# Attention and feed-forward on one core: eight sink keys in place of sixteen, and one transposed sink tile for two pairs of heads

## The chip, the cores and the metric

One core of a Trainium2 chip runs the whole program in one launch. The metric is the device time of one execution in microseconds (us). The 128 x 128 matrix engine is TensorE, shown as PE in the profile, with its weight loads shown apart as PEld. VectorE is DVE, ScalarE is ACT, GpSimd is POOL, and SyncE is SP, whose queue issues all the transfers.

## The reference

```python
scores = q @ k.T / sqrt(64)                # 4 batches, 8 heads, 768 positions, head size 64
keep   = (key < n_sink) | ((0 <= query - key) & (query - key < window))   # n_sink 4, window 128
a      = exp(scores - max) over the kept keys; a = a / (sum(a) + 1e-9)
x      = (a @ v), heads side by side       # 3072 tokens x 512
h      = x @ w_in                          # 512 x 2048
g      = s * max(h, 0)**2 + b
out    = g @ w_out                         # 2048 x 512
```

So each query block of 128 sees its own key block, the one before it, and the first four keys, the sinks. All is 32-bit float.

## The kernel before, in words

The 3072 tokens are eight chunks of 384 (`ORDER`: a batch and a half of its sequence). While TensorE does the feed-forward of chunk c, the attention of chunk c + 1 is laid between its steps. A value that needs more than TensorE's fast 32-bit form keeps is split into a high part and a rest, so one product costs two or three matmuls.

**The feed-forward** (`moe_steps`) of a chunk has 32 steps: for each of 16 slices f, `l1(f)` makes `h` with 12 matmuls of 384 columns (L598), and `l2(f)` adds nine matmuls of 512 columns into three output banks (L617). Between them ScalarE takes the relu into tile `r` (L601), VectorE squares it in place (L603), ScalarE makes the high part of `g` (L605) and VectorE the rest (L606), which is the last reader of `r`. `l2(f)` stands two slices behind `l1(f)`. `r` has two buffers.

**Attention.** Chunks 0 and 1 use a plain form. Chunks 2 to 7 use the blocked form, whose work is cut into slots, one for each unit: a head and a block of 128 queries, 24 units a chunk, two heads to a pair. `unit_a` makes scores of 272 columns: two key blocks and 16 sink keys between or after them (144 for the first block of a sequence), with two matmuls, `kh` (L303) and `kl` (L304). VectorE masks and takes the maximum (L308), ScalarE the exponential (L314), GpSimd adds the two key blocks into one (L317) and copies the sinks' exponentials three times into `psk` (L318). A few slots later `turn` transposes the sum (L324), `unit_b` parts and splits it (L337 to L340), and `unit_c` multiplies with the values (L368, L376).

**Sinks and 1/sum.** The sinks' part of the output and the factor 1/sum come for a whole pair at once. `psk` holds, for the three query blocks of a pair, the sinks' exponentials (96 rows after the transpose) and 1/sum in two parts (rows 96 to 99). At the end of a pair, three transposes bring it into bank `ts` (L390), ScalarE and VectorE move it to `xsk` (L392, L393). `sinks` then does one matmul `os` with the sink values `vs` (L399), `scaled` one matmul `zb` with the selector `sel` (L406), and L407 to L409 write the pair's `x`, which the next chunk's `l1` reads.

**What sets the order.** `attn_slots` writes down in which slot each piece stands: `LB` and `LC` slots after a unit's scores, and `LD` or, for the last pair, `LDL` for `sinks` and `scaled`. The loop at the end of the file deals the slots out over the steps by the line below, so that a step takes one slot or, here and there, two. A scheduler may still move instructions that do not depend on each other.

```python
            while i < len(slots) and i * (len(steps) - 2 * (c > 0)) < (j + 1) * len(slots):
```

The banks `sc`, `o`, `ts`, `os`, `zb` and `h` go round in one pool of five.

Of the kernel before, what the change touches and what calls it, by code (L numbers as in the profile page):

```python
# [40 lines left out]
def tile_kernel(ctx, tc, qT, kT, k0, v, vsk, n_sink, window, w, s, b, out):  # L41
# [15 lines left out]
    m_all = const.tile([P, 6 * P], MDT, tag="m", name="m_all")  # L57
# [30 lines left out]
    sel = const.tile([P, P], F32R, tag="sel", name="sel")  # L88
# [44 lines left out]
    def constants2():  # L133

        spread = wk.tile([P, P], F32, tag="y", name="spread", bufs=2)
        nc.gpsimd.memset(spread, 0.0)
        for j in range(2):
            nc.gpsimd.affine_select(
                out=spread[96:P].rearrange("p (a d) -> p a d", a=2), in_=spread[96:P].rearrange("p (a d) -> p a d", a=2),
                pattern=[[1, 2], [0, D]], compare_op=ALU.not_equal, fill=1.0, base=2 * j, channel_multiplier=-1)  # L140
# [98 lines left out]
    def load_pair(k, pr):  # L239
# [4 lines left out]
        nkb, k0, kw, v0 = 3 + half, (0, 288)[half], (416, 544)[half], half * 2  # L244
# [28 lines left out]
    def prep_head(k, h):  # L273
# [6 lines left out]
        hd.kh = wk.tile([P, 544], F32R, tag="kh", name="kh")  # L280
        hd.kl = wk.tile([P, 544], F32R, tag="kl", name="kl")
# [10 lines left out]
    def unit_a(k, h, i, sc):  # L292
# [25 lines left out]
        nc.gpsimd.tensor_copy(out=pp.psk[:, i, :6 * NS].rearrange("p (t x) -> p t x", t=3)[:, :, hh * NS:(hh + 1) * NS],  # L318
# [7 lines left out]
    def unit_b(k, h, i, tp):  # L326
# [18 lines left out]
        if h % 2 == 1 and i == BLK - 1:  # L345
            zr = wk.tile([P, 2, BLK, 2], F32, tag="zr", name="zr")
# [4 lines left out]
            nc.gpsimd.tensor_copy(out=pp.psk[:, :, 96:98], in_=zh.bitcast(F32))  # L351
            nc.vector.tensor_tensor(out=pp.psk[:, :, 98:100], in0=zr[:, 1], in1=zh.bitcast(F32), op=ALU.subtract)

    def unit_c(k, h, i):
# [24 lines left out]
        if i == BLK - 1:  # L379
            a, c = (0, D) if h % 2 == 0 else (D, 0)  # L380
            if h % 2 == 0:
                pp.x = wk.tile([P, CH + P], F32, tag="y", name="y", bufs=2)
            nc.scalar.copy(pp.x[a:a + D], hd.o[c:c + D])
            nc.vector.tensor_tensor(out=pp.x[a:a + D], in0=hd.o[a:a + D], in1=pp.x[a:a + D], op=ALU.add)
            if h % 2 == 1:
                nc.gpsimd.tensor_tensor(out=pp.x[:, CH - P:CH], in0=pp.x[:, CH - P:CH], in1=pp.x[:, CH:], op=ALU.add)
# [4 lines left out]
                pp.xs = wk.tile([P, CH], F32R, tag="xsk", name="xsk", bufs=1)
# [10 lines left out]
    def scaled(k, pr):  # L402
# [8 lines left out]
    def attn_slots(c):  # L411
        k = new_chunk(c)
        units, ahead = [], {}
        for pr in range(H // 2):
# [172 lines left out]
    def moe_steps(x, store, wk, before=None, last=False):  # L587
# [3 lines left out]
        def l1(f):  # L591
# [179 lines left out]
    for c in range(NC_):  # L771
# [5 lines left out]
        for j, st in enumerate(steps):  # L777
# [56 lines left out]
```

## Time and profile before

| | |
|---|---|
| Median of 3 runs | 738.36 us (737.77 to 741.83) |
| The profiled execution, its own time | 739.34 us |
| Its span in the profile | 737.2 us |
| Mean granted TensorE clock | 0.977 |
| TensorE matmuls, busy | 704.9 us (96%) |
| VectorE, ScalarE, GpSimd busy | 516.1, 480.0, 396.3 us (70%, 65%, 54%) |

The profiled execution took 2.1 us more than its span: that lies before the first and behind the last instruction of the program. Matmuls overlap in the profile (the end of one is modelled and lies behind the start of the next), so the time that one takes from the next is read from start to start, or from the chain of work that ended last, and not from its own length.

### The profile page before, as it was taken

To read this page: it belongs to the slowest core of one execution; us is meant where nothing else is said; L and a number is where in the kernel's file an instruction comes from. 1 tells how busy PE (TensorE), PEld (TensorE's weight loads), DVE (VectorE), ACT (ScalarE), POOL (GpSimd) and SP (SyncE) were. 2 spreads that over 40 slices of the span, in tenths; PEclk is the share of its full clock that TensorE was granted. 3 is DMA by queue.
4 is the path that set the end of the run, shared out by engine and by line. 5 is a ranking of instruction groups with operands and counts; after the bars stand their busy time and mean duration, and the time that the engine had idled before them with its cause. 6 is when DMAs were issued, how large, how long until landed. Compare 5 with 4: busy or idle time off the path is not lost.

```text
span 737.2 us, 11878 instructions
## 1 busy us (share of the span) xinstructions
PE 704.9 (96%) x3848; PEld 622.0 (84%) x3848; DVE 516.1 (70%) x1213; ACT 480.0 (65%) x1169; POOL 396.3 (54%) x641
## 2 busy tenths in 40 slices
PE   6788899899999999999999999999999999999996
PEld 3367677789988999999998999999999999989895
DVE  6779999738984788757785588847886589743331
ACT  5978888568774787656884677746775677633222
POOL 2254555348991689616773589816775389710000
PEclk9879989999999999999999999999999999999998
DMA  7844122041210212111121222111111212000001
GB/s 280 337 171 193 33 102 72 15 139 51 80 63 31 84 55 65 34 61 54 46 64 44 82 63 64 46 54 49 56 53 45 84 42 59 12 18 26 1 1 47
DMA packets 27221, 53.01 MB, mean 72 GB/s; under 512 B 3472, under 2 KB 15376, under 8 KB 25232
## 3 DMA queue, kind: packets, MB, share of 16 engines
q1 hardware_dynamic: 27152, 52.18, 21.2%
q8 instruction: 32, 0.52, 0.3%
q14 instruction: 37, 0.30, 0.1%
HBM read 45.88 MB, written 6.29 MB: 71 GB/s over the span
## 4 chain that ended last, share of the span: by engine, by line
PE 79%; DVE 10%; DMA 3%; ACT 3%; POOL 2%; issue 1%; SPq 1%; POOLq 0%; ACTq 0%; DVEq 0%
PE po L617 32%; PE h L598 32%; PE o L376 3%; PE sc L303 2%; PE sc L304 2%; PE sc L324 2%; DMA vf<-in_v 2%; DMA w<-in_w 2%; DVE w L214 2%; DVE g L606 1%; DVE wt L213 1%; PE ts L390 1%; POOL w L216 1%; DVE smf L528 1%; DVE r L603 1%
## 5 line engine op out<-in xcount | busy, mean ns | idle before, releaser
L598 PE MATMUL h<-x,w 128*128 128x384 f32 x1536 | 299.8, 344 | 1.1 <-ACT tf L542 0.8
L617 PE MATMUL po<-w,g 128*128 128x512 f32 x1152 | 298.0, 404 | 0.0
L598 PEld LDWEIGHTS h<-x,w 128*128 128x128 f32 x1536 | 268.6, 189 | 6.7 <-ACT tf L542 1.1
L617 PEld LDWEIGHTS po<-w,g 128*128 128x128 f32 x1152 | 212.4, 191 | 45.0 <-issue 2.7
L603 DVE SCALAR_TENSOR_TENSOR r<-h,sb,r 128x384 f32<-128x384 f32 x128 | 78.6, 614 | 82.5 <-ACT r L601 82.2
L606 DVE SCALAR_TENSOR_TENSOR g<-r,sb,g 128x384 fp32r<-128x384 f32 x128 | 102.0, 797 | 39.0 <-ACT g L605 38.2
L340 POOL TENSOR_TENSOR hl<-two,hl 128x256 fp32r<-128x256 f32 x128 | 99.3, 776 | 21.4 <-ACT hl L339 18.2
L601 ACT ACTIVATE r<-h 128x384 f32<-128x384 f32 x128 | 62.3, 487 | 66.7 <-PE h L598 66.5
L605 ACT ACTIVATE g<-r,sb 128x384 fp32r<-128x384 f32 x128 | 78.7, 615 | 34.1 <-DVE r L603 32.8
L317 POOL TENSOR_TENSOR sm<-sm 128x128 f32<-128x128 f32 x128 | 68.0, 531 | 59.5 <-ACT sm L314 55.5
L314 ACT ACTIVATE sm<-sm,negm 128x272 f32<-128x272 f32 (+1 forms) x144 | 73.1, 507 | 35.4 <-DVE negm L308 31.0
L308 DVE CUSTOM_DVE_ANT_0 sm<-sc,msk 128x272 f32<-128x272 f32 (+1 forms) x144 | 60.4, 419 | 40.4 <-PE sc L304 32.6
L284 POOL TENSOR_TENSOR kl<-kraw,kh 128x544 fp32r<-128x544 f32 (+1 forms) x48 | 63.1, 1315 | 21.7 <-ACT kh L282 21.7
L339 ACT CAST hl<-two 128x256 fp32r<-128x256 f32 x128 | 50.6, 395 | 31.6 <-DVE two L337 31.6
L216 POOL TENSOR_TENSOR w<-w 128x1024 int32<-128x1024 int32 (+1 forms) x17 | 32.6, 1919 | 45.6 <-DVE w L214 25.1
L337 DVE TENSOR_TENSOR two<-sc,split 128x256 f32<-128x256 f32 x128 | 53.0, 417 | 4.4 <-POOL hl L340 4.2
L318 POOL COPY psk<-sm 128x48 f32<-128x48 f32 x144 | 40.7, 282 | 26.7 <-ACT sm L314 26.1
L289 POOL TENSOR_TENSOR vv<-vraw,vv 128x256 fp32r<-128x256 f32 (+1 forms) x48 | 34.4, 718 | 24.6 <-ACT vv L288 24.6
L376 PE MATMUL o<-hl,vv 128*128 128x256 f32 (+1 forms) x256 | 44.5, 276 | 0.0
L303 PE MATMUL sc<-kh,qs 128*128 128x272 f32 (+1 forms) x144 | 42.6, 298 | 0.0
L376 PEld LDWEIGHTS o<-hl,vv 128*128 128x128 f32 x256 | 39.6, 189 | 2.9
L304 PE MATMUL sc<-kl,qs 128*128 128x272 f32 (+1 forms) x144 | 41.3, 288 | 0.0
(129 smaller groups left out, 904.4 us busy)
## 6 DMA issues: line engine op xcount, KB each, us to landing
w<-in_w SPq DMA_DIRECT2D x15, 1024.0 KB, 9.0
kraw<-in_kT SPq DMA_DIRECT2D x32, 272.0 KB, 2.6
out<-ot SPq DMA_DIRECT2D x24, 256.0 KB, 2.0
qraw<-in_qT SPq DMA_DIRECT2D x24, 192.0 KB, 2.4
vraw<-in_v SPq DMA_DIRECT2D x16, 256.0 KB, 2.7
kraw<-in_kT SPq DMA_DIRECT2D x16, 208.0 KB, 2.4
vsraw<-in_vsk SPq DMA_DIRECT2D x24, 64.0 KB, 2.0
vraw<-in_v SPq DMA_DIRECT2D x8, 192.0 KB, 2.4
```

What stands on the lines that cost most here:

```text
L284: nc.gpsimd.tensor_tensor(out=hd.kl[:, :kw], in0=hd.k[:, :kw], in1=hd.kh[:, :kw].bitcast(F32), op=ALU.subtract)
L308: nc.vector.tensor_tensor_reduce(out=sm[:, :n], in0=sc[:, :n], in1=m, scale=-0.125, scalar=BIG, op0=ALU.add, op1=ALU.min, accum_out=negm[: ...
L314: nc.scalar.activation(sm[:, :n], sm[:, :n], AF.Exp, bias=negm[:, uu], scale=-1.0, accum_out=pp.zz[:, i, hh:hh + 1])
L317: nc.gpsimd.tensor_tensor(out=sm[:, c1:c1 + P], in0=sm[:, p1:p1 + P], in1=sm[:, c1:c1 + P], op=ALU.add)
L340: nc.gpsimd.tensor_tensor(out=lo, in0=both, in1=hi.bitcast(F32), op=ALU.subtract)
L376: nc.tensor.matmul(hd.o[:, q0:q0 + n * P], hd.vv[:, kb, :], hd.hl[:, t, c0 * P:(c0 + n) * P], start=(hd.n == 0), stop=(i == BLK - 1 and kb ...
L598: nc.tensor.matmul(h[:, :CH], weight[f][:, 0, wi, cc * P:(cc + 1) * P], x[xi][:, cc, :], start=(i == 0), stop=(i == 11))
L601: nc.scalar.activation(r, h[:, :CH], AF.Relu, scale=1.0 / WUP)
L603: nc.vector.scalar_tensor_tensor(out=r, in0=h[:, :CH], scalar=sw_ap, in1=r, op0=ALU.mult, op1=ALU.mult)
L605: nc.scalar.activation(gg[:, 0, :], r, AF.Identity, bias=b_ap, scale=1.0)
L606: nc.vector.scalar_tensor_tensor(out=gg[:, 1, :], in0=r, scalar=b_ap, in1=gg[:, 0, :].bitcast(F32), op0=ALU.add, op1=ALU.subtract)
L617: nc.tensor.matmul(po[tb], gg[:, gi, tsl], weight[f][:, 1, wi, :], start=(f == 0 and i == 0), stop=(f == NF - 1 and i == 2))
```

## The change

The blocked form now keeps eight sink keys for each head. Scores have 264 columns (136 for the first block), and the score masks, key loads and the sinks' share of `psk` shrink with them. Two pairs now share one `psk`: the sinks' exponentials of four heads fill the 96 rows that two heads filled, and 1/sum of four heads fills rows 96 to 103. So the three transposes, the bank `ts` and its two moves come once for two pairs; `sel` becomes two selectors. `sinks` and `scaled` of a pair wait for the second pair of its two, `LD` and `LDL` give each of the two its own slots, and `load_sinks` moves from two slots ahead of a pair to eleven behind its start. The pairs' `x` tiles (`y`) have three buffers, and `r` has one; in the first chunk's feed-forward every second `r` takes the buffer of `xsk`. Chunks 1 to 6 have 34 slots for 29 of the 32 steps; they had 33 for 30.

```diff
-NS = 16
+NS = 8
-RB, VB = 2, 2
+RB, VB = 1, 2
-LB, LC, LD, LDL, L2 = 4, 7, (3, 4), (2, 2), 2
+LB, LC, LD, LDL, L2 = 4, 7, ((3, 4), (6, 7)), ((2, 2), (3, 3)), 2
...
-    sel = const.tile([P, P], F32R, tag="sel", name="sel")
+    sel = const.tile([P, 2, P], F32R, tag="sel", name="sel")
...
-        pp.psk = psks[(k.c * (H // 2) + pr) % 2]
+        pp.psk = psks[(k.c * (H // 4) + pr // 2) % 2]
...
-            c0, n = ((0, 272), (128, 272), (272, 272))[i]
+            c0, n = ((0, W), (P, W), (W, W))[i]
...
-        nc.gpsimd.tensor_copy(out=pp.psk[:, i, :6 * NS].rearrange("p (t x) -> p t x", t=3)[:, :, hh * NS:(hh + 1) * NS],
+        nc.gpsimd.tensor_copy(out=pp.psk[:, i, :12 * NS].rearrange("p (t x) -> p t x", t=3)[:, :, h % 4 * NS:(h % 4 + 1) * NS],
...
-                pp.x = wk.tile([P, CH + P], F32, tag="y", name="y", bufs=2)
+                pp.x = wk.tile([P, CH + P], F32, tag="y", name="y", bufs=3)
...
+            if h % 4 == 3:
                 ts = ps("ts")
                 for j in range(BLK):
                     nc.tensor.transpose(ts[:, j * P:(j + 1) * P], pp.psk[:, j, :], ident)
-                pp.xs = wk.tile([P, CH], F32R, tag="xsk", name="xsk", bufs=1)
+                pp.xs = k.pairs[h // 2 - 1].xs = wk.tile([P, CH], F32R, tag="xsk", name="xsk", bufs=1)
...
-        nc.tensor.matmul(zb[:, :CH], sel, pp.xs, start=True, stop=True)
+        nc.tensor.matmul(zb[:, :CH], sel[:, pr % 2], pp.xs, start=True, stop=True)
...
-            todo = ((-5, load_pair, pr), (-5, load_keys, h), (-2, load_sinks, pr), (-2, prep_head, h), (-2, load_keys, h + 1),
+            todo = ((-5, load_pair, pr), (-5, load_keys, h), (11, load_sinks, pr), (-2, prep_head, h), (-2, load_keys, h + 1),
...
-            t = 2 * BLK * (pr + 1) - 1 + LC
-            for d, fn in zip(LD if pr < H // 2 - 1 else LDL, (sinks, scaled)):
+            t = 4 * BLK * (pr // 2 + 1) - 1 + LC
+            for d, fn in zip((LD if pr < H // 2 - 2 else LDL)[pr % 2], (sinks, scaled)):
...
-            r = wk.tile([P, CH], F32, tag="r", name="r", bufs=RB)
+            r = wk.tile([P, CH], F32, tag="xsk" if before and f % 2 else "r", name="r", bufs=RB)
...
-            while i < len(slots) and i * (len(steps) - 2 * (c > 0)) < (j + 1) * len(slots):
+            while i < len(slots) and i * (len(steps) - 3 * (c > 0)) < (j + 1) * len(slots):
```

Three places show how instructions now stand on an engine. Lines in the changed kernel are numbered two higher from L347 on (L392 is the transposes' L390, L401 and L408 are `os` and `zb`, L600 and L619 are `l1` and `l2`).

TensorE, in the middle of a chunk, where the first pair of heads ends; before:

```order
L368 MATMUL o<-hl,vv 128x256
L376 MATMUL o<-hl,vv 128x256 x2
L390 MATMUL ts<-identr,psk_96 128x128 x3
L303 MATMUL sc<-kh,qs 128x272
L304 MATMUL sc<-kl,qs 128x272
L324 MATMUL sc<-identr,sm 128x128
```

In the changed kernel, TensorE a little later in the same chunk, where the first pair's `os` and `zb` (sinks and 1/sum) now stand, in a step that takes two slots:

```order
L377 MATMUL o<-hl,vv 128x256 x2
L377 MATMUL o<-hl,vv 128x128 x2
L303 MATMUL sc<-kh,qs 128x264
L304 MATMUL sc<-kl,qs 128x264
L324 MATMUL sc<-identr,sm 128x128
L369 MATMUL o<-hl,vv 128x256
L377 MATMUL o<-hl,vv 128x256 x2
L303 MATMUL sc<-kh,qs 128x264
L304 MATMUL sc<-kl,qs 128x264
L401 MATMUL os<-xsk,vs 128x384
L324 MATMUL sc<-identr,sm 128x128
L600 MATMUL h<-x_2_1391,w_944 128x384
```

The transposes of the first pair are gone (its `psk` is turned with the second pair's), and its `os` stands behind two slots that follow each other without a feed-forward step between them.

TensorE at the end of a chunk, behind the 12 matmuls of `l1` for the last slice but those named; before:

```order
L617 MATMUL po<-w_1132,g 128x512 x9
L399 MATMUL os<-xsk,vs 128x384
L406 MATMUL zb<-xsk,sel 128x384
L617 MATMUL po<-w_1193,g 128x512 x9
L617 MATMUL po<-w_1267,g 128x512 x9
L598 MATMUL h<-x_3_2485,w_415 128x384
```

In the changed kernel (the last pair's `os` and `zb` and what follows, up to the next chunk's first `l1`):

```order
L600 MATMUL h<-x_2_1391,w_1271 128x384
L401 MATMUL os<-xsk,vs 128x384
L408 MATMUL zb<-xsk,sel 128x384
L619 MATMUL po<-w_1136,g 128x512 x9
L619 MATMUL po<-w_1197,g 128x512 x9
L619 MATMUL po<-w_1271,g 128x512 x9
L600 MATMUL h<-x_3_2475,w_419 128x384
```

Three runs of nine `l2` matmuls now lie between the last `zb` and the next chunk's `l1`, where two lay.

ScalarE at the start of a chunk, from the relu of slice 1 to that of slice 2 (`r`), with the casts of the sink values (`vs`); before:

```order
L601 ACTIVATE r<-h 128x384
L279 CAST qs<-qraw 64x384
L270 CAST vs<-vsraw 128x128
L314 ACTIVATE sm,zz<-sm,negm 128x272
L605 ACTIVATE g<-r,sb 128x384
L282 CAST kh<-kraw 128x544
L601 ACTIVATE r<-h 128x384
```

In the changed kernel:

```order
L603 ACTIVATE r<-h 128x384
L279 CAST qs<-qraw 64x384
L314 ACTIVATE sm,zz<-sm,negm 128x264
L282 CAST kh<-kraw 128x528
L607 ACTIVATE g<-r,sb 128x384
L270 CAST vs<-vsraw 128x128 x2
L603 ACTIVATE r<-h 128x384
```

The relu of slice 2 stands behind both first casts of sink values, where before one of them stood ahead of it and one behind. It now writes the one buffer of `r`, which slice 1 has to leave first.

## Rows read from the trace of the kernel before

**Rows 1.** The page: busy time of each engine; the chain that ended last, by engine.

```profile
PE 704.9 (96%) x3848; PEld 622.0 (84%) x3848; DVE 516.1 (70%) x1213; ACT 480.0 (65%) x1169; POOL 396.3 (54%) x641
PE 79%; DVE 10%; DMA 3%; ACT 3%; POOL 2%; issue 1%; SPq 1%; POOLq 0%; ACTq 0%; DVEq 0%
```

**Rows 2.** Busy us by stage: window, length, PE, PEld, DVE, ACT, POOL, clock, DMA.

```profile
0.00:54.00 54.00, 39.98 (x201) 24.09 (x202) 38.92 (x135) 39.13 (x91) 18.88 (x28) 0.84 0.69 265
54.00:133.00 79.00, 68.25 (x347) 53.54 (x345) 76.63 (x130) 62.68 (x120) 42.08 (x26) 0.93 0.26 96
133.00:234.53 101.53, 101.18 (x561) 91.21 (x561) 71.51 (x167) 68.59 (x173) 65.77 (x110) 0.98 0.22 66
234.53:320.27 85.74, 85.67 (x486) 78.73 (x485) 63.78 (x150) 59.08 (x151) 59.30 (x103) 1.00 0.19 57
320.27:403.56 83.29, 83.29 (x469) 76.52 (x469) 59.38 (x150) 56.30 (x151) 47.90 (x87) 1.00 0.18 57
```

**Rows 3.** The chain that ended last, 234 to 326 us: start, us, what.

```profile
261.21 0.24 PE o L376 x2
...
267.58 0.33 PE ts L390 x3
267.91 0.12 PE sc L303
268.03 0.13 PE sc L304
268.16 0.11 PE sc L324
...
320.09 0.18 PE zb L406
320.27 4.18 PE po L617 x18
```

**Rows 4.** The chain again, 324 to 332 us, where a 144-column pair stands.

```profile
326.56 0.07 PE sc L303
326.63 0.11 PE sc L304
326.74 0.17 PE sc L303
326.91 0.13 PE sc L304
```

**Rows 5.** TensorE in order of time: start, length, line, operation.

```profile
296.99 0.29 PE L304 MATMUL sc<-kl,qs 128*128 128x272 f32 x1
297.36 0.33 PE L324 MATMUL sc<-identr,sm 128*128 128x128 f32 x1
```

**Rows 6.** Groups by line: busy us, mean ns | idle before, releaser.

```profile
L598 PE MATMUL h<-x,w 128*128 128x384 f32 x1536 | 299.8, 344 | 1.1 <-ACT tf L542 0.8 <-DVE xsk L393 0.3
L393 DVE TENSOR_TENSOR xsk<-ts,xsk 32x384 fp32r<-32x384 f32 x24 | 13.2, 550 | 0.7
L407 DVE TENSOR_TENSOR y<-zb,y 128x384 f32<-128x384 f32 x24 | 13.2, 548 | 0.6
L408 ACT CAST x<-y 128x384 fp32r<-128x384 f32 x24 | 12.2, 510 | 20.2 <-DVE y L407 20.1
L409 DVE TENSOR_TENSOR x<-y,x 128x384 fp32r<-128x384 f32 x6 | 3.4, 558 | 3.8 <-ACT x L408 3.8
L392 ACT CAST xsk<-ts 128x384 fp32r<-128x384 f32 x24 | 11.5, 480 | 0.6
```

**Rows 7.** ScalarE and VectorE in order of time, start of a chunk.

```profile
246.03 0.48 ACT L601 ACTIVATE r<-h 128x384 f32<-128x384 f32 x1
250.85 0.49 ACT L601 ACTIVATE r<-h 128x384 f32<-128x384 f32 x1 [0.78 <-PE h L598]
...
245.63 0.68 DVE L606 SCALAR_TENSOR_TENSOR g<-r,sb,g 128x384 fp32r<-128x384 f32 x1
247.88 0.77 DVE L606 SCALAR_TENSOR_TENSOR g<-r,sb,g 128x384 fp32r<-128x384 f32 x1 [0.69 <-ACT g L605]
```

More of the change, by code (lines that the diff above doesn't have):

```diff
@@ L56, in tile_kernel @@
     late = []
-    m_all = const.tile([P, 6 * P], MDT, tag="m", name="m_all")
+    m_all = const.tile([P, 6 * P + NS], MDT, tag="m", name="m_all")
     m_full = [m_all[:, a * P:(a + j + 1) * P] for j, a in ((0, 0), (1, 1), (2, 3))]
@@ L67, in tile_kernel @@
     split = const.tile([P, 2, P], U8, tag="split", name="split")
-    msk = const.tile([P, 3 * W + P + NS], MDT, tag="msk", name="msk")
-    m_1, m_odd, m_even = (msk[:, j * W:(j + 1) * W] for j in range(3))
-    m_0 = msk[:, 3 * W:]
+    msk = const.tile([P, 2 * W + P + NS], MDT, tag="msk", name="msk")
+    m_1, m_even = (msk[:, j * W:(j + 1) * W] for j in range(2))
+    m_odd, m_0 = m_all[:, 4 * P:], msk[:, 2 * W:]
     warm = first.tile([P, 512], mybir.dt.bfloat16, tag="warm", name="warm")
@@ L133, in constants2 @@
     def constants2():
-        spread = wk.tile([P, P], F32, tag="y", name="spread", bufs=2)
+        spread = wk.tile([P, 2, P], F32, tag="y", name="spread", bufs=3)
         nc.gpsimd.memset(spread, 0.0)
[L137 to L140, printed above, removed]
+        for j in range(4):
+            row = spread[96:P, j // 2].rearrange("p (a d) -> p a d", a=2)
+            nc.gpsimd.affine_select(out=row, in_=row, pattern=[[1, 2], [0, D]], compare_op=ALU.not_equal, fill=1.0,
+                                    base=2 * j, channel_multiplier=-1)
         nc.scalar.copy(sel, spread)
@@ L153, in constants2 @@
         mask(m_even[:, P:P + NS], snk[:, :NS])
+        mask(m_odd[:, 2 * P:], snk[:, :NS])
         cp = nc.gpsimd.tensor_copy
@@ L156, in constants2 @@
         cp(out=m_0[:, NS:], in_=lom)
-        for m, l0 in ((m_1, P), (m_even, P + NS), (m_odd, P)):
+        for m, l0 in ((m_1, P), (m_even, P + NS)):
             cp(out=m[:, :P], in_=upm)
             cp(out=m[:, l0:l0 + P], in_=lom)
-        cp(out=m_odd[:, 2 * P:], in_=m_even[:, P:P + NS])
     NU = B * H * 2 * BLK
@@ L243, in load_pair @@
         half = k.half
-        nkb, k0, kw, v0 = 3 + half, (0, 288)[half], (416, 544)[half], half * 2
+        nkb, k0, kw, v0 = 3 + half, (0, 2 * P + 2 * NS)[half], (3 * P + 2 * NS, 4 * P + 2 * NS)[half], half * 2
         pp.q = wk.tile([P, CH], F32, name="qraw", tag="qraw", bufs=1)
@@ L279, in prep_head @@
         nc.scalar.copy(hd.qs[hd.half], hd.q)
-        hd.kh = wk.tile([P, 544], F32R, tag="kh", name="kh")
-        hd.kl = wk.tile([P, 544], F32R, tag="kl", name="kl")
+        hd.kh = wk.tile([P, 4 * P + 2 * NS], F32R, tag="kh", name="kh")
+        hd.kl = wk.tile([P, 4 * P + 2 * NS], F32R, tag="kl", name="kl")
         nc.scalar.copy(hd.kh[:, :kw], hd.k[:, :kw])
@@ L345, in unit_b @@
         if h % 2 == 1 and i == BLK - 1:
+            z0 = 12 * NS + h // 2 % 2 * 4
             zr = wk.tile([P, 2, BLK, 2], F32, tag="zr", name="zr")
@@ L350, in unit_b @@
             nc.vector.tensor_copy(zh, zr[:, 1])
-            nc.gpsimd.tensor_copy(out=pp.psk[:, :, 96:98], in_=zh.bitcast(F32))
-            nc.vector.tensor_tensor(out=pp.psk[:, :, 98:100], in0=zr[:, 1], in1=zh.bitcast(F32), op=ALU.subtract)
+            nc.gpsimd.tensor_copy(out=pp.psk[:, :, z0:z0 + 2], in_=zh.bitcast(F32))
+            nc.vector.tensor_tensor(out=pp.psk[:, :, z0 + 2:z0 + 4], in0=zr[:, 1], in1=zh.bitcast(F32), op=ALU.subtract)
     def unit_c(k, h, i):
@@ L447, in slot @@
             return f
-        return k, [slot(t) for t in range(n + LC + LDL[1])]
+        return k, [slot(t) for t in range(n + LC + LDL[1][1])]
     class Plain:
@@ L812 @@
     vsk = np.zeros((B, H // 2, P, P), v.dtype)
-    for t in range(3):
-        for hh in range(2):
-            r0 = t * 2 * NS + hh * NS
-            vsk[:, :, r0:r0 + NS, hh * D:(hh + 1) * D] = v[:, hh::2, :NS]
+    for t, pr, hh in np.ndindex(3, H // 2, 2):
+        r0 = (t * 4 + pr % 2 * 2 + hh) * NS
+        vsk[:, pr, r0:r0 + NS, hh * D:(hh + 1) * D] = v[:, 2 * pr + hh, :NS]
     w_in, w_out = np.asarray(inputs["moe_w_in"]), np.asarray(inputs["moe_w_out"])
```

6 lines of the change are left out of this document (3 added, 3 removed).

## The prediction

> **What bounds the kernel now.** I read the page first. TensorE is busy 96% of the span and makes 79% of the chain that ended last [rows 1]. A busy matmul engine may still be waiting, so I went to the stages. Up to 133 us TensorE has gaps (68.25 of 79 us in the second stage), and VectorE, at 76.63 of 79, is the fuller engine [rows 2]; that stage makes the weights and runs the plain attention. From 133 us on the picture turns: TensorE is busy 101.18 of 101.53, then 85.67 of 85.74 and 83.29 of 83.29 us, at a granted clock of 0.98 to 1.00, which is its 2.4 GHz level [rows 2]. The blocked attention, which the change touches, lies in this part, in six chunks. Its chain, read piece by piece, is matmul after matmul without a gap [rows 3]. So a column or a matmul removed there is worth the time that it takes from the next one, and work removed from another engine is worth nothing until that engine makes TensorE wait.
>
> **Transposes.** Three transposes of `psk` take 0.33 us of the chain, and the matmuls around them take no less for it: the scores and the transpose behind them show the same 0.12, 0.13 and 0.11 us as everywhere [rows 3]. They go at two of the four pairs in each of six chunks: 12 x 0.33 = 3.96 us. This is the main term, and the surest.
>
> **Scores.** 256 of the 288 score matmuls go from 272 to 264 columns, the other 32 from 144 to 136. A 272-column one takes 0.12 to 0.13 us, mean 0.125, and an `o` matmul of 256 columns 0.24 / 2 = 0.12 [rows 3]: 0.005 us over 16 columns, some 0.3 ns a column. A 512-column one takes 4.18 / 18 = 0.232 us [rows 3], so from 272 to 512 it is 0.107 / 240 = 0.45 ns a column. Eight columns are 2.5 to 3.6 ns. I take 3.6, since the second slope rests on the larger difference: 256 x 3.6 ns = 0.92 us. For the 32 short ones I take nothing: the pair of 144 columns and the pair of 272 behind it take 0.07 + 0.11 + 0.17 + 0.13 = 0.48 us [rows 4], against 0.50 for two pairs of 272, so 256 columns fewer gave 0.02 us. There something other than columns sets the pace, and the lower bound for the whole cut is 0.
>
> The Trainium skill (TensorE: Matmul & The Clock Gate, Back-to-back issue gap) speaks against both terms. It gives the spacing in a stream of weight loads and matmuls as about 81 ns at 128 columns and 131 at 512. By its figures, as an estimate, 36 transposes would be worth 2.9 us and the cut 0.3, together 3.2. The trace of this kernel's 32-bit operands differs, with 0.11 us for 128 columns and 0.232 for 512 [rows 3], and the trace decides.
>
> **What leaves the other engines.** At 12 of 24 pairs ScalarE loses the 480 ns move and VectorE the 550 ns one [rows 6], and GpSimd's copies get shorter. None of it is on the chain, so I count it as 0, with one exception. TensorE's `l1` matmuls waited 0.3 us in all on VectorE's `xsk` move [rows 6]; that move is gone at half of the pairs, and I count a gain of 0.3, at the least 0.
>
> **The later end of a pair.** `os`, `zb` and L407 to L409 of a pair come later, so the question is whether the next chunk's `l1` would now wait for the last pair's `x`. Behind `zb` VectorE, ScalarE and VectorE take 548 + 510 + 558 ns = 1.6 us [rows 6]. TensorE had 18 `l2` matmuls of 4.18 us to cover that [rows 3], and the changed order has 27, or 6.27 us. The third pair's `zb` stands even an `l1` ahead of this. The cost is 0; without that cover it would be at most 1.6 us in each of six chunks.
>
> **One buffer of `r`.** The relu of slice f + 1 must now wait until L606 of slice f has ended. It queues behind nothing new on VectorE; behind it on ScalarE stand exponentials and the high part of `g`. At the start of a chunk, where three `l1` steps come close together, the relu of slice 2 began at 246.03 and L606 of slice 1 ended at 245.63 + 0.68 = 246.31 us [rows 7]: it will start 0.28 us later. The next relu began at 250.85, and L606 of its forerunner ended at 248.65 us [rows 7], so there are 2.2 us to spare. The delay is caught up before `l2` of that slice, two slices on, needs its `g`, and five banks stand between `h` and its reuse. I take 0. Without that cover the 0.28 us would come once in each of the seven chunks with one `r` buffer: 2.0 us.
>
> **Loads and small things.** The casts of the sink values now stand as two ahead of the relu of slice 2; the values are needed many steps later, and their loads still stand in SP's queue at the start of the chunk, the third of them now behind a key load that it stood ahead of. The key loads are 3% shorter. The stage up to 133 us keeps its order on every engine but for a few constants; there `r` alternates between two buffers as before. I take 0 for all.
>
> **Steps with two slots.** A chunk has five steps with two slots (34 slots in 29 steps) where it had three. A second slot needs a bank soon after the first. In the trace one such step waits: at 297.36 us a transpose starts 0.37 us after the matmul ahead of it [rows 5], where 0.13 is usual [rows 3], so 0.24 us are lost, in a place where `os`, `zb` and `h` hold banks as well. The step with two slots at 267 us shows no wait [rows 3]. In the changed order the step with `os` at the first pair's end is crowded in the same way, in all six chunks; before, three had it. I count 3 x 0.24 = 0.7 us lost; at the best 0.
>
> **The sum.** -3.96 - 0.92 - 0.3 + 0.7 = -4.5 us. For the profiled execution that is a span of 732.7 and a time of 734.8 us. Its 739.34 stands 0.98 above the median of the runs shown, so against the median I forecast 738.36 - 4.5 = 733.9 us, 0.6% less. Less than 0.5% (3.7 us) of this kernel can hardly be told from no change.
>
> **The rivals.**
>
> *Columns are free.* If weight loads pace the 272-column scores as they pace the 144-column ones [rows 4], the score cut is worth 0 and the time is 734.8 us. Against it: 272 columns take longer than 256 [rows 3], if by little. The spacing of the Trainium skill's page named above points the same way, and further: as an estimate 735.6 us, with its 3.2 us in place of the two terms.
>
> *The gain is given back in waits.* ScalarE and VectorE get a denser middle of the chunk: the same 24 units in one step fewer. If the relu's 0.28 us reaches TensorE in seven chunks (2.0) and two more two-slot steps in each chunk wait 0.24 us (2.9), the time is 733.9 + 4.9 = 738.8 us, no change; half of that gives 736.3. For it: VectorE has 63.78 us of work in a chunk of 85.74 [rows 2], and nearly all of the attention stands in the first three quarters. Against it: each chunk also loses 2 x 550 ns there [rows 6].
>
> *A bank wait at every two-slot step.* It is the mechanism of 297.36 us, grown: with `os`, `zb` and `h` waiting in VectorE's queue, a transpose waits for a bank for as long as VectorE needs for a whole move, and the five steps of a chunk all meet it. The move of `zb` is 548 ns [rows 6]; at all 30 places that is 16.4 us, less the 0.7 that I count already, and the time is 749.6 us. It is slower than before by over 0.5% once the 30 places lose (4.5 + 3.7) / 30 = 0.27 us each beyond what I count. Against it: the chain from 240 to 296 us runs without a gap through the other such steps [rows 2, 3].
>
> **How the numbers follow.** I give the forecast 0.58, free columns 0.13, waits that give back half or more 0.21, and the bank wait 0.08. The forecast itself lies between 732.5 us (no bank wait left, 0.7 us of them gone instead of added) and 735.2 us. The range over the cases is 731.8 to 738.0 us: its low end is that 732.5 less the 0.6 us between the median and the lowest run, and it holds the first two cases and most of the third. Under 734.67 us, faster by over 0.5%, lie most of the forecast and about half of the second case: 0.57. Slower by over 0.5% is the bank wait alone: 0.07. Within 0.5%: 0.36.
>
> **What would show it.** Right: 36 transposes L392 in place of 72 and 0.33 us less at two pairs of a chunk in the chain; the stage of a chunk 0.6 to 0.8 us shorter (85.74 to about 84.9, 83.29 to about 82.7); scores at 0.12 us; the stages up to 133 us and from 658.30 us as long as before. Wrong: relus that end a wait on L608 with TensorE's `l1` or `l2` waiting behind them; transposes L324 that start over 0.3 us after the score ahead of them at more than one place of a chunk; `l1` of a new chunk waiting for `x`; or a first stage that has moved by more than 1 us.

## The result, and the profile after

The changed kernel took 748.15 us, median of 4 runs (747.03 to 748.92), against 739.24 us for the kernel before in the same comparison. The ratio is 1.0116, 95% interval 1.0082 to 1.015: slower, where 733.9 us was forecast. The profiled execution took 748.66 us, with a span of 746.9.

The page of the changed kernel, its busy line and the chain that ended last, answers to [rows 1]:

```profile
PE 702.7 (94%) x3812; PEld 615.4 (82%) x3812; DVE 518.8 (69%) x1202; ACT 474.2 (63%) x1157; POOL 388.9 (52%) x640
PE 54%; DVE 24%; ACT 8%; issue 5%; DMA 4%; POOL 3%; SPq 1%; ACTq 0%; POOLq 0%; DVEq 0%
```

TensorE has 36 matmuls and 2.2 us of busy time less, as the change promised. But only 54% of the chain is TensorE's now (79% before), and 24% VectorE's (10% before). TensorE waits. For whom, the view of its waits shows (who waits, for whom: us in total, times, longest), and two groups by line beside [rows 6]:

```profile
PE h L600 <- DVE two L337: 8.9, 11, 1.0
...
PE sc L324 <- DVE y L385: 2.8, 4, 0.7
```

```profile
L600 PE MATMUL h<-x,w 128*128 128x384 f32 x1536 | 297.6, 343 | 10.1 <-DVE two L337 8.9 <-ACT tf L544 0.9
...
L392 PE MATMUL ts<-identr,psk 128*128 128x128 f32 x36 | 5.9, 272 | 0.0
```

Where: the first `l1` of chunk 1 begins at 151.97 us (152.11 before), the last chunk's first `l1` 74.2 us before the end (74.9). So all of the loss lies between. I measure a **stage** from a chunk's first `l1` to that of the next. The six stages were 86.45, 85.73, 83.30, 85.77, 83.28 and 85.68 us, 510.2 in all; now they are 88.31, 88.11, 84.35, 87.82, 84.64 and 87.51, 520.7. The windows of the second and the third (length, then PE, PEld, DVE, ACT, POOL busy, clock, DMA) answer to the last two of [rows 2]:

```profile
240.28:328.40 88.12, 85.59 (x480) 77.67 (x479) 64.32 (x147) 58.06 (x150) 58.10 (x103) 1.00 0.18 55
328.40:412.74 84.34, 83.19 (x464) 75.62 (x463) 59.61 (x147) 55.33 (x150) 46.76 (x87) 1.00 0.18 55
```

TensorE is idle for 2.5 us in the first of these, where it was idle for 0.07. Its timeline shows three places (start, length, what; `l1` for slice 7, the transpose behind slice 9's `l1`, `l1` for slice 10):

```profile
272.76 0.27 PE L324 MATMUL sc<-identr,sm 128*128 128x128 f32 x1
274.00 0.79 PE L600 MATMUL h<-x,w 128*128 128x384 f32 x3 [0.97 <-DVE two L337]
...
287.63 0.28 PE L304 MATMUL sc<-kl,qs 128*128 128x264 f32 x1
288.61 0.30 PE L324 MATMUL sc<-identr,sm 128*128 128x128 f32 x1 [0.70 <-DVE y L385]
...
292.44 0.27 PE L324 MATMUL sc<-identr,sm 128*128 128x128 f32 x1
293.45 0.77 PE L600 MATMUL h<-x,w 128*128 128x384 f32 x3 [0.74 <-DVE two L337]
```

From start to start 1.24, 0.98 and 1.01 us, where 0.03, 0.12 and 0.03 are usual: 1.2, 0.9 and 1.0 us lost. By the code, an `l1` reads weights and `x`, and a transpose reads `sm`: nothing that L337 or L385 makes. What these VectorE instructions still hold is one of the five banks, as its last readers. And why VectorE is late, the chain before the first place tells, which was matmul after matmul in [rows 3]:

```profile
267.45 0.52 ACT qs L279
267.97 0.02 issue
267.99 1.55 DVE qs L283
...
269.57 0.34 DVE zr L349
269.91 0.02 issue
269.93 0.20 DVE zr L350
270.13 0.02 issue
270.15 0.59 DVE zh L351
270.75 0.02 issue
270.77 0.17 DVE psk L353
270.94 0.53 DVE r L605
271.47 0.34 DVE sm L308
...
271.85 0.69 DVE y L385
272.54 0.03 issue
272.57 0.92 DVE g L608
273.49 0.03 issue
273.52 0.44 DVE two L337
273.96 0.04 issue
274.00 1.15 PE h L600 x5
```

For six microseconds VectorE is never idle: the subtraction for the next head's `qs` and the four operations of 1/sum stand in its queue ahead of four reads of banks. Behind a pair's end TensorE reaches a place where it wants a bank at once, and waits. So my theory was: **TensorE loses the time where it wants a bank early while VectorE is late with its reads.** The two-slot steps bear on the first half of that. The changed kernel has them at steps 0, 5, 11, 17 and 23 of a chunk, the kernel before at 0, 10 and 20. From step 2 on, even steps are an `l1` and odd ones an `l2`. Two slots behind an `l2` are followed by an `l1`, which wants a bank; behind an `l1` they are followed by nine `l2` matmuls, 2.1 us that want none. (Step 0 is an exception in both kernels: the second `l1` follows it.) Rivals: the single buffer of `r` (R); the place alone, so that two slots at an odd step cost and at an even step don't, whatever VectorE does (P1); and the number of two-slot steps alone, whatever their place (P2).

### The profile page after: what moved, and what is told of

The parts are those of the page before. It is cut to its first block, busy times and chain, and to the rows that moved or that the text cites. A ratio compares the mean times of both kernels' runs of the same rounds, so it can differ in the third digit from the quotient of the medians.

```text
span 746.9 us, 11840 instructions
## 1 busy us (share of the span) xinstructions
PE 702.7 (94%) x3812; PEld 615.4 (82%) x3812; DVE 518.8 (69%) x1202; ACT 474.2 (63%) x1157; POOL 388.9 (52%) x640
## 4 chain that ended last, share of the span: by engine, by line
PE 54%; DVE 24%; ACT 8%; issue 5%; DMA 4%; POOL 3%; SPq 1%; ACTq 0%; POOLq 0%; DVEq 0%
PE h L600 24%; PE po L619 23%; DVE g L608 4%; DVE qs L283 3%; DVE r L605 2%; PE o L377 2%; DVE two L337 2%; DVE sm L308 2%; DMA vf<-in_v 2%; DVE w L214 2%; DMA w<-in_w 2%; ACT sm L314 2%; DVE wt L213 1%; ACT g L607 1%; ACT r L603 1%
## 5 line engine op out<-in xcount | busy, mean ns | idle before, releaser
L600 PE MATMUL h<-x,w 128*128 128x384 f32 x1536 | 297.6, 343 | 10.1 <-DVE two L337 8.9
L619 PE MATMUL po<-w,g 128*128 128x512 f32 x1152 | 297.0, 404 | 0.0
L600 PEld LDWEIGHTS h<-x,w 128*128 128x128 f32 x1536 | 266.9, 189 | 18.9 <-PE sc L324 6.5
L619 PEld LDWEIGHTS po<-w,g 128*128 128x128 f32 x1152 | 212.3, 191 | 46.1 <-issue 2.8
L608 DVE SCALAR_TENSOR_TENSOR g<-r,sb,g 128x384 fp32r<-128x384 f32 x128 | 107.6, 841 | 44.2 <-ACT g L607 43.2
L605 DVE SCALAR_TENSOR_TENSOR r<-h,sb,r 128x384 f32<-128x384 f32 x128 | 78.8, 615 | 76.4 <-ACT r L603 75.3
L607 ACT ACTIVATE g<-r,sb 128x384 fp32r<-128x384 f32 x128 | 78.9, 617 | 49.8 <-DVE r L605 49.6
L317 POOL TENSOR_TENSOR sm<-sm 128x128 f32<-128x128 f32 x128 | 69.1, 540 | 71.6 <-ACT sm L314 68.7
L340 POOL TENSOR_TENSOR hl<-two,hl 128x256 fp32r<-128x256 f32 x128 | 97.2, 762 | 12.8 <-ACT hl L339 12.0
L314 ACT ACTIVATE sm<-sm,negm 128x264 f32<-128x264 f32 (+1 forms) x144 | 72.0, 500 | 36.0 <-DVE negm L308 35.0
L284 POOL TENSOR_TENSOR kl<-kraw,kh 128x528 fp32r<-128x528 f32 (+1 forms) x48 | 60.2, 1253 | 19.5 <-ACT kh L282 18.7
L337 DVE TENSOR_TENSOR two<-sc,split 128x256 f32<-128x256 f32 x128 | 53.0, 418 | 2.2 <-POOL hl L340 1.1
L318 POOL COPY psk<-sm 128x24 f32<-128x24 f32 x144 | 34.6, 240 | 23.0 <-ACT sm L314 23.0
L377 PE MATMUL o<-hl,vv 128*128 128x256 f32 (+1 forms) x256 | 45.1, 276 | 0.7 <-POOL hl L340 0.7
L308 DVE CUSTOM_DVE_ANT_0 sm<-sc,m_all 128x264 f32<-128x264 f32 x64 | 27.2, 425 | 26.5 <-PE sc L304 24.9
L283 DVE TENSOR_TENSOR qs<-qraw,qs 64x384 fp32r<-64x384 f32 x48 | 42.1, 878 | 4.0 <-ACT qs L279 2.3
L377 PEld LDWEIGHTS o<-hl,vv 128*128 128x128 f32 x256 | 39.5, 188 | 4.2 <-POOL hl L340 1.5
L308 DVE CUSTOM_DVE_ANT_0 sm<-sc,msk 128x264 f32<-128x264 f32 (+1 forms) x80 | 31.7, 398 | 15.9 <-PE sc L304 14.5
```

What stands on the lines that cost most here:

```text
L308: nc.vector.tensor_tensor_reduce(out=sm[:, :n], in0=sc[:, :n], in1=m, scale=-0.125, scalar=BIG, op0=ALU.add, op1=ALU.min, accum_out=negm[: ...
L314: nc.scalar.activation(sm[:, :n], sm[:, :n], AF.Exp, bias=negm[:, uu], scale=-1.0, accum_out=pp.zz[:, i, hh:hh + 1])
L317: nc.gpsimd.tensor_tensor(out=sm[:, c1:c1 + P], in0=sm[:, p1:p1 + P], in1=sm[:, c1:c1 + P], op=ALU.add)
L337: nc.vector.tensor_tensor(out=both.rearrange("p (s c) -> p s c", s=2), in0=tp.unsqueeze(1).to_broadcast([P, 2, P]), in1=split, op=ALU.mult)
L340: nc.gpsimd.tensor_tensor(out=lo, in0=both, in1=hi.bitcast(F32), op=ALU.subtract)
L377: nc.tensor.matmul(hd.o[:, q0:q0 + n * P], hd.vv[:, kb, :], hd.hl[:, t, c0 * P:(c0 + n) * P], start=(hd.n == 0), stop=(i == BLK - 1 and kb ...
```

## The experiments

The part up to 152 us took 149.2 to 154.9 us in these runs, though most edits do not touch it. Single executions are therefore compared by the sum of their six stages; in the one kernel that was traced twice the two sums are 505.94 and 505.89 us.

| kernel | time, us | six stages, us |
|---|---|---|
| before (profiled execution) | 739.34 | 510.2 |
| changed (profiled execution) | 748.66 | 520.7 |
| b_r1, before with one `r` | 736.9 | 511.1 |
| b_pace3, before, 33 slots in 29 steps | 745.75 | 516.9 |
| b_odd, before, two slots at 0, 11, 21 | 752.76, ratio 1.018 (1.0142 to 1.0218) | 525.7 |
| b_ns8, before with eight sink keys | 736.89 | 508.6 |
| a_pace2, changed, 34 slots in 30 steps | 739.34 | 507.9 |
| a_33of30, changed, 33 slots in 30 steps | 732.63 | 505.9 |
| a_33of30_t, the same again | 732.52, ratio 0.9914 (0.9881 to 0.9947) | 505.9 |
| a_even5, changed, two slots at even steps | 744.26, ratio 1.0063 (1.004 to 1.0085) | 516.5 |
| a_late2, changed, two slots at 24 to 28 | 743.39 | 512.4 |
| a_noeps, changed, one VectorE operation less | 741.11 | 512.3 |
| a_zpool, changed, 1/sum mostly on GpSimd | 746.46 | 515.7 |
| a_33of30_4banks, a_33of30 with four banks | 745.34 | 516.1 |
| a_qspool, changed, `qs` on GpSimd | 741.72 | 516.6 |
| a_33of30_qspool, a_33of30, `qs` on GpSimd | 742.98 | 515.4 |

**One part of the change alone.** b_r1 gives the kernel before the changed kernel's buffers of `r`:

```diff
-RB, VB = 2, 2
+RB, VB = 1, 2
-            r = wk.tile([P, CH], F32, tag="r", name="r", bufs=RB)
+            r = wk.tile([P, CH], F32, tag="xsk" if before and f % 2 else "r", name="r", bufs=RB)
```

> The kernel before with one buffer of r alone (in the first chunk every second r takes the buffer of xsk). Theory P (steps with two slots: five in a chunk against three, and a bank is wanted before VectorE has left it): about the time before, 738 to 740 us, chunk stages of 85.7 and 83.3 us. Theory R (the single r: the relu waits, VectorE's moves come later and the banks with them): most of the 9 us loss, 745 to 749 us, chunk stages 1.5 us longer.

Five of the six stages stay within 0.07 us of before, the first is 0.74 longer. R falls.

b_pace3 gives the kernel before the changed kernel's pacing, and a_pace2 and a_33of30 give the changed kernel that of before; a_33of30 also has 33 slots instead of 34:

```diff
-            while i < len(slots) and i * (len(steps) - 3 * (c > 0)) < (j + 1) * len(slots):
+            while i < len(slots) and i * (len(steps) - 2 * (c > 0)) < (j + 1) * len(slots):
```
```diff
-LB, LC, LD, LDL, L2 = 4, 7, ((3, 4), (6, 7)), ((2, 2), (3, 3)), 2
+LB, LC, LD, LDL, L2 = 4, 7, ((3, 4), (6, 7)), ((2, 2), (2, 2)), 2
```

> The kernel before with its 33 slots dealt over 29 steps instead of 30 (four steps with two slots), nothing else. Theory P: slower by some 3 to 9 us, with bank waits of 0.5 to 1.2 us behind steps with two slots. Theory R: within 1 us of before.

> The changed kernel with its 34 slots dealt over 30 steps instead of 29 (four steps with two slots instead of five). Theory P: part of the loss comes back, 740 to 745 us. Theory R: 747 to 749 us as the changed kernel.

> The changed kernel with the slots of before: the last two pairs' sinks and 1/sum all in slot 32, so 33 slots, dealt over 30 steps (three steps with two slots, as before). Theory P: the waits go and the 4.9 us of TensorE work shows, 733 to 736 us. Theory R: 746 to 749 us. If the sharing of one psk itself is at fault (the later ends of pairs): in between, with waits at the os and zb of the pairs.

> The changed kernel with 33 slots in 30 steps again, timed in rounds: steps with two slots at 0, 10 and 20, as before. P1 and P2 both: 732 to 735 us, faster than before by 0.6 to 0.9%.

The pacing alone costs the kernel before 6.7 us of its stages, and taking it out of the changed kernel gives 12.8 back, with the 34th slot 14.8. Two-slot steps now stand at 0, 7, 14 and 21 in b_pace3 and at 0, 7, 15 and 22 in a_pace2, two of them behind an `l2` in each; a_pace2 lies only 2.0 us above a_33of30. a_33of30 has two-slot steps at 0, 10 and 20 again and is faster than both kernels: the ratio of 0.9914 is 6.4 us. Its second and third stage in the windows:

```profile
236.95:322.21 85.26, 84.75 (x479) 77.69 (x478) 62.64 (x147) 58.14 (x150) 58.19 (x103) 1.00 0.20 56
322.21:404.46 82.25, 82.25 (x464) 75.44 (x462) 59.04 (x147) 55.24 (x150) 47.25 (x87) 1.00 0.19 57
```

In the third there is no idle time at all, and the stage is 1.05 us shorter than before. So the work that the change removes is worth what was forecast; the loss lies in how the slots are dealt out.

**Number or place.** b_odd moves two of the three two-slot steps of the kernel before by one step, a_even5 puts the five of the changed kernel at even steps, a_late2 puts them at the end:

```diff
-            while i < len(slots) and i * (len(steps) - 2 * (c > 0)) < (j + 1) * len(slots):
+            while i < len(slots) and (c == 0 and i * len(steps) < (j + 1) * len(slots) or c > 0 and i <= j + sum(j >= t for t in (0, 11, 21))):
```

(a_even5 has `(0, 6, 12, 18, 24)` in it, a_late2 `j + max(j - 23, 0)`.)

> The kernel before with its steps with two slots at 0, 11 and 21 instead of 0, 10 and 20: the same number, the latter two moved from behind an l1 to behind an l2. P1: slower by 1 to 2 us a chunk, 745 to 750 us. P2: as before, 738 to 741 us.

> The changed kernel with its 34 slots in 29 steps, but the five steps with two slots put at 0, 6, 12, 18 and 24, each behind an l1, where the changed kernel has 0, 5, 11, 17 and 23, four of them behind an l2. Theory P1 (what costs is a step with two slots behind an l2: the next step is an l1, which wants a bank at once, while behind an l1 the next step is an l2, which wants none): the loss goes, 732 to 736 us. Theory P2 (the number of steps with two slots costs, wherever they stand): 746 to 749 us as the changed kernel.

> The changed kernel with its 34 slots in 29 steps, the five steps with two slots at 24 to 28, where no new scores are made and VectorE has less to do. P1: 24, 26 and 28 cost nothing, 25 and 27 lie behind an l2, but VectorE is not late there, so little: 732 to 737 us. P2: 746 to 749 us.

P2 falls: b_odd has three two-slot steps as before and loses 15.5 us in the stages, more than the changed kernel with five. Its TensorE at slice 7, in order of time (the scheduler has also put a third slot's scores and three of the nine `l2` matmuls ahead of `l1` there):

```profile
272.19 0.29 PE L304 MATMUL sc<-kl,qs 128*128 128x272 f32 x1
272.31 0.86 PE L617 MATMUL po<-w,g 128*128 128x512 f32 x3
274.94 1.29 PE L598 MATMUL h<-x,w 128*128 128x384 f32 x6 [1.77 <-DVE y L384]
```

This wait, 1.6 to 2.1 us, comes in each of the six stages; in the last of them the granted clock was also 0.50, the 1.2 GHz level, behind it (622.2 to 625.4 us), and the 12 `l1` matmuls took 3.7 us instead of 2.2. At slice 12, behind the other moved step, only 0.3 to 0.4 us are lost. So the place alone does not decide.

P1 is only half right in the other runs too. In a_even5 the waits of `l1` at slices 7 and 10 are nearly gone, as P1 has it, but that of the transpose behind slice 9, at a step with a single slot, grew from 0.9 to 1.6 us in chunk 2; of the 10.5 us lost it gets back 4.3. In a_late2 one wait is left, 1.5 to 2.0 us (0.3 in the last stage) at slice 13's transpose, a two-slot step behind an `l1`; P1 had expected 732 to 737 us. The two waits, a_even5 first:

```profile
288.58 0.30 PE L324 MATMUL sc<-identr,sm 128*128 128x128 f32 x1 [1.41 <-DVE y L385]
```
```profile
310.32 0.30 PE L324 MATMUL sc<-identr,sm 128*128 128x128 f32 x1 [1.32 <-DVE r L605]
```

An even step is no safe place where VectorE is late.

**VectorE's lateness.** a_noeps leaves out the addition of 1e-9 to the sum, one small VectorE operation for each pair, and a_zpool moves three of the four operations of 1/sum to GpSimd. Places and banks stay:

```diff
-            nc.vector.tensor_scalar(out=zr[:, 0], in0=pp.zz, scalar1=1e-9, scalar2=None, op0=ALU.add)
-            nc.vector.reciprocal(out=zr[:, 1], in_=zr[:, 0])
+            nc.vector.reciprocal(out=zr[:, 1], in_=pp.zz)
```
```diff
-            nc.vector.tensor_scalar(out=zr[:, 0], in0=pp.zz, scalar1=1e-9, scalar2=None, op0=ALU.add)
+            nc.gpsimd.tensor_scalar(out=zr[:, 0], in0=pp.zz, scalar1=1e-9, scalar2=None, op0=ALU.add)
...
-            nc.vector.tensor_copy(zh, zr[:, 1])
+            nc.gpsimd.tensor_copy(zh, zr[:, 1])
...
-            nc.vector.tensor_tensor(out=pp.psk[:, :, z0 + 2:z0 + 4], in0=zr[:, 1], in1=zh.bitcast(F32), op=ALU.subtract)
+            nc.gpsimd.tensor_tensor(out=pp.psk[:, :, z0 + 2:z0 + 4], in0=zr[:, 1], in1=zh.bitcast(F32), op=ALU.subtract)
```

> The changed kernel without the addition of 1e-9 to the sum of exponentials ahead of the reciprocal: one small operation of VectorE less at each pair's end, the order and the banks as in the changed kernel. VectorE theory (TensorE waits for a bank that VectorE has not yet read out, since it is late behind the operations of 1/sum and the subtraction of qs): the waits of slices 7 and 9, which stand behind a pair's end, shrink by the time of that one operation, 0.2 to 0.5 us each, so that the time falls by 2 to 6 us to 743 to 746 us. If the places of the two-slot steps alone decide, with VectorE's load of no weight, nothing changes: 748 us within 1 us.

> The changed kernel with the addition, the copy and the subtraction around the reciprocal of 1/sum on GpSimd, so that VectorE keeps only the reciprocal of the four. VectorE theory: VectorE comes 0.6 to 1.2 us earlier to the two L337 and to L385 at slices 7 and 9, each of these waits shrinks by about that, and the time is 737 to 743 us; but the reciprocal now waits for GpSimd's addition, and whatever stands behind it in VectorE's queue waits too, so that a GpSimd that is late gives part of it back. If VectorE's lateness is not the cause: 748 us within 1 us, or more.

a_noeps gets back 8.4 us, more than the 2 to 6 expected, by 24 operations, 20 of which took 0.3 to 0.4 us each and all together 9.7 us. The same stretch of VectorE as in the chain above, in a_noeps (L604 to L607 are the others' L605 to L608):

```profile
267.70 1.37 DVE L283 TENSOR_TENSOR qs<-qraw,qs 64x384 fp32r<-64x384 f32 x1 [0.26 <-ACT qs L279]
269.10 0.19 DVE L349 RECIPROCAL zr<-zz 128x6 f32<-128x6 f32 x1
...
269.54 0.74 DVE L352 TENSOR_TENSOR psk<-zr,zh 128x6 f32<-128x6 f32 x1
...
271.92 0.62 DVE L607 SCALAR_TENSOR_TENSOR g<-r,sb,g 128x384 fp32r<-128x384 f32 x1
272.57 0.42 DVE L337 TENSOR_TENSOR two<-sc,split 128x256 f32<-128x256 f32 x1
```

From the start of L283 to that of L337 4.87 us pass, 5.53 in the changed kernel; TensorE's wait at slice 7 shrinks from 1.2 to 0.5 us, and that at slice 9 is nearly gone; that at slice 10 stays at 0.9. So the same places cost 6.4 us over a_33of30 in place of 14.8 once VectorE is 0.7 us earlier. a_zpool takes the wait at slice 7 down to 0.14 us, but 1/sum now queues on GpSimd, whose L340 comes later: matmuls of `o` (L377) wait 5.3 us in all for it, 0.7 in the changed kernel. It gets back 5.1 us, and its 746.46 us miss the 737 to 743 expected.

**Why VectorE is late.** L283 takes 0.55 to 1.55 us for the same 64 x 384 elements, the copy L351 0.17 to 0.7 for six columns. GpSimd in the stretch of the chain above, changed kernel:

```profile
267.80 1.32 POOL L284 TENSOR_TENSOR kl<-kraw,kh 128x528 fp32r<-128x528 f32 x1
269.09 0.78 POOL L317 TENSOR_TENSOR sm<-sm 128x128 f32<-128x128 f32 x1
269.81 0.19 POOL L318 COPY psk<-sm 128x24 f32<-128x24 f32 x1
269.97 0.73 POOL L340 TENSOR_TENSOR hl<-two,hl 128x256 fp32r<-128x256 f32 x1
```

L283 began at 267.99, while L284 ran, and ended at 269.54, 0.42 us after the end of L284 (269.12). L351 began at 270.15, while L340 ran, and ended at 270.73, 0.03 after it (270.70). Over the whole trace: of 48 L283, the 14 ahead of which no GpSimd operation was under way took 0.55 to 0.56 us, and 32 of the other 34 ended 0.41 to 0.42 us after a GpSimd operation that had begun before them. 12 of the 14 had an L317 of GpSimd begin beside them; each of these L317 ended 0.32 to 0.33 us after its L283. 23 of 24 L351 ended 0.03 to 0.04 us after a GpSimd operation that had begun before them. The Trainium skill (SBUF — State Buffer, Who interferes with whom) says that a VectorE instruction with two inputs in SBUF contends with GpSimd instructions that read SBUF, and that the one which starts second blocks until the first ends; the rows of L283 agree, on both sides. L351 has one input, so that sentence does not cover it; its rows show only that it ends with the GpSimd operation. I tested it by moving L283 behind L284 on GpSimd:

```diff
-        nc.vector.tensor_tensor(out=hd.qs[other], in0=hd.q, in1=hd.qs[hd.half].bitcast(F32), op=ALU.subtract)
+        nc.gpsimd.tensor_tensor(out=hd.qs[other], in0=hd.q, in1=hd.qs[hd.half].bitcast(F32), op=ALU.subtract)
```

> The changed kernel with the subtraction for qs (L283) on GpSimd in place of VectorE, where it stands just ahead of the subtraction for kl (L284) that it stood still for. Theory that VectorE is late because it stands still while GpSimd works: VectorE is 1.1 to 1.5 us earlier behind each of the heads' subtractions, the waits at slices 7 and 9 (1.2 and 0.9 us) go nearly to zero, and the time is 737 to 742 us. GpSimd does about 1 us more for each head, and its L340 comes later: waits of the output's matmuls on L340 may grow by up to 1 us a chunk. Theory that only the places of the two-slot steps count: 748 us within 1.5 us.

> The changed kernel with 33 slots in 30 steps (732.6 us), and the subtraction for qs on GpSimd as in a_qspool. Hardly a wait for VectorE is left in that kernel but those of slices 11 and 13 (together 0.2 to 1.4 us a chunk), so an earlier VectorE is worth at most 2 us, and a later GpSimd may cost as much where the output's matmuls wait on L340: 731 to 735 us. 745 us or more would mean that GpSimd has become the bound.

a_qspool gets back 4.1 us: the wait at slice 9 falls from 0.9 to 0.3, but that at slice 7 only from 1.2 to 1.0, not to zero as expected. VectorE in its stretch ahead of slice 7, and the two GpSimd operations beside it:

```profile
266.08 1.00 DVE L349 TENSOR_SCALAR zr<-zz 128x6 f32<-128x6 f32 x1 [0.93 <-ACT sm L314]
267.12 0.19 DVE L350 RECIPROCAL zr<-zr 128x6 f32<-128x6 f32 x1
267.35 0.83 DVE L351 CAST zh<-zr 128x6 fp32r<-128x6 f32 x1
```
```profile
265.71 1.35 POOL L284 TENSOR_TENSOR kl<-kraw,kh 128x528 fp32r<-128x528 f32 x1
267.13 1.01 POOL L283 TENSOR_TENSOR qs<-qraw,qs 64x384 fp32r<-64x384 f32 x1
```

With L283 gone, the operations of 1/sum stand still instead: six columns take 1.00 and 0.83 us, each to the end of a GpSimd operation. The stall moved in part; the standing still is shown, but the cure was a small one. a_33of30_qspool missed its expectation by 8 us. Its windows around the waits of slices 12 and 13:

```profile
305.00:307.50 2.50, 1.01 (x5) 0.68 (x5) 2.37 (x6) 1.00 (x3) 2.42 (x6) 1.00 0.34 103
307.50:309.00 1.50, 1.26 (x5) 1.26 (x6) 1.15 (x4) 1.26 (x3) 0.86 (x2) 0.71 0.00 0
309.00:312.00 3.00, 3.00 (x13) 3.00 (x12) 1.15 (x2) 0.81 (x3) 2.14 (x3) 0.58 0.00 0
312.00:316.00 4.00, 4.00 (x22) 3.59 (x21) 1.91 (x3) 1.61 (x4) 0.60 (x1) 1.00 0.00 0
```

VectorE and GpSimd are full (2.37 and 2.42 of 2.50 us), TensorE worked 1.01 of 2.50, and after that its granted clock fell (0.71 and 0.58 in the next two windows, and 0.50, its 1.2 GHz level, from 308.2 to 311.4 us): the 12 `l1` matmuls of slice 13 took 3.72 us from the first's start to the start of what follows (307.74 to 311.46), in place of 2.2. The same happened at slice 13 of chunk 4 and nowhere else in the six stages; in these two the waits are paid twice.

**Banks and columns.** a_33of30_4banks takes one bank from the fast version:

```diff
-    psA = ctx.enter_context(tc.tile_pool(name="psA", bufs=5, space=bass.MemoryType.PSUM))
+    psA = ctx.enter_context(tc.tile_pool(name="psA", bufs=4, space=bass.MemoryType.PSUM))
```

> The changed kernel with 33 slots in 30 steps (732.6 us) and four banks in the pool in place of five. If TensorE waits for banks that VectorE has yet to read out, a bank less makes each wait begin one bank earlier: waits of 0.5 us or more at several places of every chunk, and 745 us or more in all. If a bank is free long before it is wanted except at the odd two-slot steps, the time stays within 2 us of 732.6.

It loses 10.2 us in the stages, in waits for VectorE's reads (of its view of waits):

```profile
PE sc L324 <- DVE r L605: 4.6, 8, 0.8
...
PE h L600 <- DVE r L605: 1.6, 1, 1.6
```

The waits come without any change of VectorE's work or of the slots' places, so a bank too few does what an early demand does. b_ns8 is the kernel before with eight sink keys alone (a change of `NS` and of the offsets that follow from it; its `xsk` rows 32 to 63 do not fit this layout, so the sinks' share of the output is another one):

```diff
-NS = 16
+NS = 8
```

> The kernel before with eight sink keys, so scores of 264 and 136 columns, and nothing else changed: the transposes, the slots and their places stay. (Sinks beyond the eighth are left out, which the mask would have dropped anyway.) If columns set the pace of the scores, each blocked chunk is 0.10 to 0.15 us shorter (40 to 48 score matmuls by 2.5 to 3.6 ns), for example 83.30 becomes about 83.16 us, and 0.6 to 0.9 us are gained in all. If weight loads set the pace ('Columns are free'), the chunks stay within 0.05 us of the kernel before.

The score matmuls follow each other after 126 ns before and 123 ns in b_ns8 (from start to start of L303 and L304, median of the 128 pairs of 272 and 264 columns), and from start to start all score matmuls of a stage take 0.14 to 0.20 us less, 1.0 us in the six. "Columns are free" falls. The stages themselves met neither expectation: the third and the fifth, where 0.10 to 0.15 us less was expected, are 0.14 and 0.19 us longer, the other four 0.45 to 0.54 shorter, 1.6 us less in all. From start to start, the `l1` matmuls of every stage take about 0.2 us less, and in the third and the fifth the transposes L324 and the `o` matmuls take 0.5 us more. Why is open.

## Why the prediction was wrong, point by point

**Steps with two slots: the step that failed.** It counted 0.7 us ("I count 3 x 0.24 = 0.7 us lost; at the best 0"). The same removed work without the new places (a_33of30) makes the stages 505.9 us, with them 520.7: 14.8 us. The reason that stood behind the small number was that the two-slot steps of [rows 3] and the stretch from 240 to 296 us showed no wait. True, but the two-slot steps of that kernel behind its chunk's start, 10 and 20, stood behind an `l1`, so that an `l2` which wants no bank followed; four of the changed kernel's five stand behind an `l2`, and two of these four wait in every chunk, before slices 7 and 10. The rows were evidence on a different kind of place. b_odd shows that the kernel before had the same weakness, one step away. (The wait of 297.36 us, which the prediction found in three chunks, stands in four of the six stages of before, at 0.36 us from start to start each time; and the low end of the range, 732.5 less 0.6, is 731.9.)

**The rival that came nearest** is "A bank wait at every two-slot step", with 749.6 us, a mechanism of the right kind: a matmul waits for a bank until VectorE has come to the read. But its price was one move of 548 ns at all 30 places; measured are 0.9 to 1.2 us at slices 7, 9 and 10 in four of the chunks (7 and 10 by the two-slot steps ahead of them, 9 without one), in the other two 0.3 to 0.6, 0.2 and 1.2, and 0.4 or less elsewhere but once in the first. I weighed VectorE by its busy share of a stage [rows 2], when what counts is how late it is at one moment: six microseconds without a gap behind a pair's end, partly because it stands still for GpSimd.

**The gain is given back in waits**: the waits are there, but the relu's 0.28 us had no part in them (b_r1).

**Right in the main**: the transposes and the columns. The third stage, free of waits in both kernels, went from 83.30 to 82.25 us in a_33of30, 1.05 less, where 0.66 for the transposes and 0.12 for its 32 scores of 272 columns were forecast. From start to start, the removed transposes give 0.57 of it, all its scores 0.22, and the `l1` matmuls, from which nothing was forecast, another 0.22. The stages together are 4.3 us shorter, with `l1` waits of 2.0 us in all left on L409. The column term (0.92) was measured at 1.0 in b_ns8. One buffer of `r` costs nothing but 0.7 us in the first stage. The later end of a pair costs nothing at the next chunk: no `l1` of a new chunk shows a wait for `x`. The part up to 152 us did not move. a_33of30 is 6.4 us faster than before, where the forecast without the two-slot steps was 5.2. That these lie close is in part luck: the gain in `l1`, some 1.4 us in the six stages, and the waits on L409 were both not forecast, and about 2 of the 6.4 us lie outside the stages.

**Open**: how much of VectorE's lateness is standing still and how much its order in the queue. In a_33of30 VectorE reads two banks (L337, L385) ahead of L283, in the changed kernel behind it, and the scheduler decides that; no run moved this order alone. What shortens the `l1` matmuls by 0.2 us a stage with eight sink keys is open too.

## What to carry to other kernels

When work is dealt out over steps, a second piece in a step is free only where the next step wants nothing from the pool that it drew on: see which kind of step each double piece stands behind, before and after, and don't take rows at one kind as evidence for the other. An engine with idle time on average can still be the bound for a microsecond: follow its queue from the burst of work to the read that frees a buffer. And a change that removes work should first be tried with the old pacing; here the old slots and pacing turned 1.2% slower into 0.9% faster.

## What the runs showed of the hardware that was not expected

A VectorE copy of six columns (L351) ended with a GpSimd operation that was under way in 23 of 24 executions of the changed kernel, and took between 0.17 and 0.70 us for it; the one that did not took 0.16. On an engine that is busy 69% of the span, 24 small operations of mostly 0.3 to 0.4 us, left out, were worth 8.4 us of the 9.7 that they had taken. And in a_33of30_qspool TensorE's granted clock went from 1.00 to 0.50, its 1.2 GHz level, after a stretch with 1.01 us of work in 2.50.
